# Two transformer layers on one core: weights in blocked layout, raw blocks read from the inputs, and part of one feed-forward step by seven products

## The chip, the cores and the metric

The kernel runs on one core of one Trainium2 chip. The metric is the device time of one execution in microseconds (us). The core has TensorE (PE, matrix products; its loads of the stationary operand are listed as PEld), VectorE (DVE), ScalarE (ACT), GpSimd (POOL, used only at the start) and SyncE (SP), which issues nearly all DMAs in program order from one queue; 16 DMA engines carry them out. PSUM has eight banks of 128 x 512 float32.

## The reference

The input x has 2048 rows of 1024 features. Two layers with the same weights are applied one after the other; each is an attention part and a feed-forward part, both with a layer norm ahead and a residual around:

```python
def _A_ref(x, wqkv, wo):                      # attention, 32 heads of 32
    qkv = (x @ wqkv).reshape(B, S, 3, H, Dh) ...
    off = jnp.arange(8) * 2                   # position s sees s, s-2, ..., s-14
    logits = einsum("bhsd,bhswd->bhsw", q, kg) * scale   # masked below 0
    o = einsum("bhsw,bhswd->bhsd", softmax(logits), vg)
    return o... @ wo

def _B_ref(x, w1, b1, w2, b2):                # feed-forward, 1024 -> 3584 -> 1024
    r = max(x @ w1 + b1, 0)
    return (r * r) @ w2 + b2

for _ in range(2):
    x = x + _A_ref(_layernorm(x), wqkv, wo)
    x = x + _B_ref(_layernorm(x), w1, b1, w2, b2)
```

All inputs are bfloat16. The products take float16 or bfloat16 operands and accumulate in float32.

## The kernel before

**Units.** The rows are split by even and odd position (so that the window of the attention is contiguous) and then into blocks of 512. A layer has four such blocks, so there are eight units, u = 0 to 7. A unit passes through these stages, each a method: SA (load four tiles of x, layer norm, transposed by DMA or, in unit 0, by PE), the projections Q, K, V, S2 (attention on DVE, ACT and a few matmuls `lg` against a constant `grp`), the output projection by wo with residual and the second layer norm, FFN1 and FFN2.

**Plain and by seven products.** A product of 512 rows is done in one of two ways. Plainly: matmuls of 512 columns, accumulated over the contraction in a PSUM bank. Or by Strassen's scheme in Winograd's form: the operands are cut in 2 x 2 blocks, and seven block products take the place of eight. Each product of FFN1, Q, K or V is then eight matmuls of 256 columns (`product`, L623, matmul at L633). They need sums and differences of activations (`rhs_combos`, tiles T and TA, made by DVE) and of weights. The products are numbered 1 to 7: numbers 1, 2 and 4 use raw weight blocks, 5, 7, 6 and 3 the four combinations s1, s3, s2, s4.

**How it is split.** Q, K and V are plain in units 0 and 1 (`SQ`, L871; the first four of K in unit 0 in halves at L858) and by seven products from unit 2 (`SQ7`). The output projection is plain in units 0, 1 and 7 (`SW`, L1053) and by seven in units 2 to 6 (`SW7`, L1124). FFN1 is plain in unit 0 (`SF1_plain`: seven blocks `dp` of four 512-column results each; L1195, relu L1203, square L1206) and by seven later (`SF1`, `ffn1_step`). FFN2 is plain in unit 0 (`SF2_plain`, L460, into all eight PSUM banks at once, each seeded with the bias by ACT at L473) and by seven later (`SF2`, L1336).

**Where the weights come from.** The plain units load them from the inputs with strided row pieces. While their weights are in SBUF, the kernel makes what the later units need and stores it to DRAM scratch: `keep_wqkv` makes the four combinations of each block on DVE (L521) from views with a stride of eight elements, copies the three raw blocks on ACT (L516, tiles `tr`), and stores all seven; `keep_w1` (L662), `keep_w2` (L433) and `keep_wo` (L1077) make combinations on DVE in tiles `tv`. The raw blocks of w1 are copied from DRAM to DRAM by 21 DMAs (`copy_w1`). `seven` then loads the scratch (`w1s`, `wqk`, `wqqv`) in tiles of four products, in the order in which they are used: one DMA of 1 MB for four products. FFN2 by seven loads combinations from `tw` and raw blocks from the input, seven pieces of 512 columns to a row. The stationary operands of Q, K and V have a stride of eight elements (plain) or two (by seven).

**FFN1 by seven, one block.** For each `dp`, `ffn1_step` uses three PSUM banks X, Y, Z. ACT copies X to Y (L571), copies X twice as `u` (in units of FOLD with the bias, L1244, two instructions each; otherwise L1240) and Z twice as `y` (L1250), takes four relus (L1277) and two squares (L1271); DVE adds u and y (L1254) and takes the maximum with zero (L1263 in units of FOLD, otherwise with the bias, L1267).

**Denominators.** In S2, `norm` sums the eight exponentials with three DVE additions (L980 to L982), or, for units in DEN, with eight matmuls by the identity in a PSUM bank; ACT takes logarithm and exponential of it.

**Order of the work.** `build` lists the operations with their data, priorities and cost estimates. `Plan.schedule` is a list scheduler: it takes, for each engine, the ready operation with the lowest priority number whose buffers are free, and the order that results is the fixed program order of each engine. ORDER holds seeds of small random shifts of the priorities; each list is one more pass. Buffers are slots of a class with a cap for each tag: 12 slots of 8 KB for a partition (`8K`; at most 8 of them weights `w`), four tiles `tv`, and so on. A DMA issue is planned at 0.08 us of SP.

Of the kernel before, what the change touches and what calls it, by code (L numbers as in the profile page):

```python
# [27 lines left out]
FOLD = (1, 2)  # L28
DEN = ()
# [20 lines left out]
NEARLY = 4  # L50
PR1 = 20.0
# [261 lines left out]
class _Kernel:  # L313
    def __init__(self, ctx, tc, x, wqkv, wo, w1, b1, w2, b2, out, n_layers=2):
# [4 lines left out]
        self.F = w1.shape[-1]  # L319
# [13 lines left out]
    def setup(self):  # L333
# [27 lines left out]
        self.wqkv_v = self.wqkv.rearrange("(kt p) n -> p kt n", p=128)  # L361
        self.wo_v = self.wo.rearrange("(p c) n -> p c n", c=self.NCH)
        self.w1_v = self.w1.rearrange("(kt p) n -> p kt n", p=128)
        self.w2_v = self.w2.rearrange("(kt p) n -> p kt n", p=128)
# [11 lines left out]
        self.wqs = {j: [tc.dram_tile([128, min(4, len(o) - i), 4, 256], F16, name=f"wq{j}{i // 4}") for i in range(0, len(o), 4)]  # L376
                    for j, o in self.orderq.items()}
        self.two = [tc.dram_tile([128, 2, 4, BLK], F16, name=f"two{i}") for i in range(2)]
        self.w1s = [tc.dram_tile([128, min(4, len(self.order1) - i), 4, 256], F16, name=f"w1s{i // 4}") for i in range(0, len(self.order1), 4)]
# [33 lines left out]
    def weights(self, ap, kt, wide=False):  # L413
        b = Buf("8K", "w", [128, 8, 512], BF)
        if wide:
            self.dma(lambda: b[:].rearrange("p (a b) n -> p a (b n)", a=4), lambda: ap, (), [(b, 0)], 1.19, name="w")
        else:
            self.dma(lambda: b[:, :kt, :], lambda: ap, (), [(b, 0)], kt * 0.145, name="w")
        return b

    def w2_block(self, k2, n2):
        h = self.KF // 2
        return self.w2_v[:, k2 * h:(k2 + 1) * h, n2 * BLK:(n2 + 1) * BLK]

    def keep_w2(self, j0, n, w):
# [3 lines left out]
        def raw(k2, n2):  # L429
            return w[:, k2, :n, n2 * BLK:(n2 + 1) * BLK]  # L430
# [9 lines left out]
    def SF2_plain(self, u):  # L440
# [7 lines left out]
        for j0 in range(0, h, 2):  # L448
            n = min(2, h - j0)
            w = Buf("8K", "w", [128, 2, 2, 2 * BLK], BF)  # L450
            for k2 in range(2):
                self.dma(lambda w=w, k2=k2, n=n: w[:, k2, :n], lambda k2=k2, j0=j0, n=n: self.w2_v[:, k2 * h + j0:k2 * h + j0 + n, :],
                         (), [(w, k2)], n * 0.285, name="w")
# [41 lines left out]
    def keep_wqkv(self, nm, ws, after=()):  # L495
# [4 lines left out]
        def one(s):  # L500
            at = {pr: i for i, (d, pr) in enumerate(self.orderq[job]) if d == (nm, s)}
# [1021 lines left out]
```

## Time and profile before

| what | value |
|---|---|
| three runs, median (lowest to highest) | 1143.3 us (1142.36 to 1145.3) |
| the profiled execution, its own time | 1144.01 us |
| its span | 1142.3 us |
| granted PE clock | 1.00 throughout |
| PE, PEld, DVE, ACT busy | 1128.2, 764.0, 1002.6, 804.6 us |
| bytes moved by DMA | 372.54 MB, 326 GB/s on the mean |
| packets | 208172, of these 68426 under 512 B and 147146 under 2 KB |

How it is read: the busy time of an engine is the sum of its instructions; matmuls overlap by their tails, so the rate of PE is taken from runs of many matmuls, not from the mean duration of one. A gap in brackets is time in which an engine did nothing, with what released it at the end. In the stretches, each line is a window of the span with the busy time and count of each engine. The queue q1 is the one that SP issues on; its share is the time that its packets took, over 16 engines and the span, and can exceed 1.0 in a window since packets overlap.

### The profile page before, as it was taken

What the parts mean: (1) busy time and instruction counts of PE and PEld (TensorE: products, weight loads), DVE (VectorE), ACT (ScalarE), POOL (GpSimd) and SP (SyncE); (2) the same over time, 40 slices, a digit from 0 to 9 for tenths busy, and PEclk for the clock granted to TensorE, in tenths of its full rate; (3) what the DMA queues carried; (4) which work ended last, traced back from release to release, by engine and by line L of the source; (5) the groups of instructions that cost most, each with busy time, mean ns of one, the idle gap of its engine ahead of it and who ended that gap; (6) DMA issues with size and microseconds to landing.
All of it is one profiled execution on the core that took longest, in us unless ns stands there. A gap on an engine that the chain in (4) does not pass through costs nothing.

```text
span 1142.3 us, 20183 instructions
## 1 busy us (share of the span) xinstructions
PE 1128.2 (99%) x7618; PEld 764.0 (67%) x7663; DVE 1002.6 (88%) x1513; ACT 804.6 (70%) x1574; POOL 1.8 (0%) x8
## 2 busy tenths in 40 slices
PE   8999999999999999999999999999999999999998
PEld 6665544568846788468874688647885578845864
DVE  7999999999997899959999699996999889996341
ACT  6965694367994689757895579946798477943861
POOL 0000000000000000000000000000000000000000
PEclk9999999999999999999999999999999999999999
DMA  9999998999999996999979998899979999688982
GB/s 347 330 311 313 328 297 274 308 358 355 392 356 375 371 372 227 338 350 349 387 275 331 409 342 299 293 339 391 360 265 311 370 369 381 242 317 275 365 296 77
DMA packets 208172, 372.54 MB, mean 326 GB/s; under 512 B 68426, under 2 KB 147146, under 8 KB 187594
## 3 DMA queue, kind: packets, MB, share of 16 engines
q1 hardware_dynamic: 207786, 370.72, 94.8%
q8 instruction: 60, 0.98, 0.3%
q10 hardware_dynamic: 288, 0.52, 0.1%
q14 instruction: 38, 0.31, 0.1%
HBM read 320.35 MB, written 41.68 MB: 317 GB/s over the span
## 4 chain that ended last, share of the span: by engine, by line
PE 68%; ACT 13%; DMA 6%; DVE 2%; issue 1%; SPq 0%; DVEq 0%; ACTq 0%
PE X L633 22%; PE Z L633 11%; PE X L1336 10%; PE Y L633 6%; PE Z L1336 5%; PE py L460 4%; PE X L1124 3%; PE py L1053 2%; PE Y L1336 2%; ACT r L1271 2%; DMA xt<-xs 2%; DMA w<-in_A_wo_dram 2%; PE Z L1124 2%; ACT rr L1277 1%; ACT r L1203 1%; ACT xn L727 1%
## 5 line engine op out<-in xcount | busy, mean ns | idle before, releaser
L633 PEld LDWEIGHTS <-w 128*128 128x128 f16 (+1 forms) x4760 | 465.7, 98 | 68.7 <-issue 0.5
L1336 PEld LDWEIGHTS <-r 128*128 128x128 f16 x1183 | 115.7, 98 | 135.7 <-issue 2.1
L1336 PE MATMUL X<-w,r 128*128 128x512 f16 (+2 forms) x784 | 177.7, 377 | 1.6 <-ACT yxa L1029 1.2
L922 DVE TENSOR_TENSOR P<-q,k 128x2048 f16<-128x2048 f16 x128 | 153.9, 1225 | 3.2 <-ACT q L848 1.6
L633 PE MATMUL X<-T,w 128*128 128x256 f16 x1176 | 147.0, 273 | 0.0
L1001 DVE TENSOR_TENSOR pr<-pb,v 128x4096 f16<-128x4096 f16 x64 | 146.3, 2295 | 0.3
L930 DVE TENSOR_TENSOR P<-P,P 128x2048 f16<-128x2048 f16 x106 | 129.5, 1222 | 0.3
L1008 DVE TENSOR_TENSOR pr<-pr 128x2048 f16<-128x2048 f16 (+1 forms) x128 | 119.0, 953 | 0.0
L1271 ACT ACTIVATE r<-rr 128x1024 f16<-128x1024 f16 x98 | 112.5, 1165 | 0.1
L633 PE MATMUL X<-TA,w 128*128 128x256 f16 x864 | 108.2, 273 | 0.2 <-ACT u L589 0.2
L571 ACT COPY Y<-X 128x512 f32<-128x512 f32 x109 | 67.5, 619 | 34.0 <-PE X L633 29.8
L871 PE MATMUL pq<-xnA,w 128*128 128x512 f16 x352 | 78.4, 379 | 0.0
L871 PEld LDWEIGHTS <-w 128*128 128x128 bf16 x352 | 50.3, 144 | 25.1
L1250 ACT CAST y<-Z 128x512 f16<-128x512 f32 x98 | 61.8, 648 | 3.7 <-PE Z L633 3.4
L1254 DVE TENSOR_TENSOR rr<-u,y 128x512 f16<-128x512 f16 x98 | 40.7, 422 | 22.0 <-ACT y L1250 11.1
L593 ACT CAST yq<-Z 128x512 f16<-128x512 f32 x72 | 41.8, 588 | 21.6 <-PE Z L633 18.8
L589 ACT CAST u<-X 128x512 f16<-128x512 f32 x72 | 42.0, 587 | 19.2 <-PE X L633 17.3
L1277 ACT ACTIVATE rr<-X,b1T 128x256 f16<-128x256 f32 x98 | 51.5, 583 | 0.5 <-PE X L633 0.3
L1277 ACT ACTIVATE rr<-Y,b1T 128x256 f16<-128x256 f32 x98 | 49.2, 539 | 3.5 <-PE Y L633 3.3
L633 PE MATMUL Z<-xnB,w 128*128 128x256 f16 x392 | 50.8, 273 | 0.0
L460 PE MATMUL py<-w,r 128*128 128x512 bf16 x219 | 48.9, 379 | 1.3 <-ACT py L473 0.9
L633 PE MATMUL Z<-T,w 128*128 128x256 f16 x392 | 50.1, 273 | 0.0
(153 smaller groups left out, 1727.1 us busy)
## 6 DMA issues: line engine op xcount, KB each, us to landing
w<-w1s SPq DMA_DIRECT2D x84, 1024.0 KB, 10.2
w<-tw SPq DMA_DIRECT2D x56, 896.0 KB, 6.4
w<-wqqv SPq DMA_DIRECT2D x42, 1024.0 KB, 10.4
w<-in_B_w_dram SPq DMA_DIRECT2D x42, 896.0 KB, 6.7
w<-wqk SPq DMA_DIRECT2D x18, 1024.0 KB, 9.2
w<-in_B_w_dram SPq DMA_DIRECT2D x28, 512.0 KB, 7.3
w<-in_A_wqkv_dram SPq DMA_DIRECT2D x12, 1024.0 KB, 11.2
w<-in_A_wo_dram SPq DMA_DIRECT2D x11, 1024.0 KB, 8.4
```

The source lines that it names most:

```text
L460: nc.tensor.matmul(bank[:], r2[:, k2 * h + j0 + j, tl * 128:(tl + 1) * 128], w[:, k2, j, n2 * BLK:(n2 + 1) * BLK], start=False, stop=(j0 + ...
L571: self.p.add("ACT", act(512), lambda: self.nc.scalar.copy(Y[:], X[:]), [(X, 0)], [(Y, 0)], UP, name="u")
L633: nc.tensor.matmul(bank[:, a, :], lw[:, k, left(a)], rhs(k), start=(start and k == 0 and a == 0), stop=(k == 3), skip_group_check=True)
L871: nc.tensor.matmul(pq[:], wv[:, kd % 4, c0:D:8], xnT[:, :, kd, :], start=(kd == 0), stop=(kd == KD - 1))
L922: nc.vector.tensor_tensor(cur[:], q[:, c, None, hb * HB:(hb + 1) * HB].to_broadcast([128, W, HB]), _win_ap(k[:, c, :], HALO + hb * HB, HB) ...
L930: nc.vector.tensor_tensor(other[:], other[:], cur[:], ALU.add)
L1001: p.add("DVE", dve(4096), lambda pr=pr, ch=ch: nc.vector.tensor_tensor(pr[:], pb[:].unsqueeze(1).to_broadcast([128, 2, W, HB]), _win_ap2(v ...
L1008: nc.vector.tensor_tensor(dst, pr[:, :, 0:n, :], pr[:, :, n:2 * n, :], ALU.add)
L1250: p.add("ACT", act(512), lambda: nc.scalar.copy(y[:], bank[:]), [(bank, 0)], [(y, 0)], 1.5, name="y")
L1271: p.add("ACT", 0.955, lambda: nc.scalar.activation(out=r2[:, f:f + 2, :].rearrange("p a t -> p (a t)"), in_=r[:].rearrange("p a m t -> p ( ...
L1277: p.add("ACT", 0.36, lambda a=a: nc.scalar.activation(out=r[:, a, 0, :], in_=bank[:, a, :], func=ACTF.Relu, bias=self.b1T[:, f + a:f + a + ...
L1336: nc.tensor.matmul(banks[q][:, lo:hi], left(jj, q), w[:, j, lo:hi], start=(start and jj == 0), stop=(jj == h - 1), skip_group_check=True)
```

## The change

- **Layout of the weights.** The host permutes wqkv, wo, w1 and w2 before the launch (`_lay`; it moves elements and computes nothing), so that every block that the kernel loads lies in long runs: 8 KB to a partition for half of Q, K or V, 4 KB for half a block of w1, 7 KB for half a block of w2, 4 KB or 8 KB for wo. In SBUF the operands of Q, K and V are then packed: the strides of eight and two are gone, from the matmuls' stationary operands and from the combinations in `keep_wqkv`.
- **Raw blocks.** The ACT copies at L516, their stores, and `copy_w1` are removed. The scratch holds combinations only. `seven` loads each raw block of a tile with its own DMA of 256 KB from the input (2 KB to a partition) and the combinations of the tile with one more; a product waits for its own piece, not for the whole tile.
- **FFN1 of unit 0.** Blocks 0 to 3 remain plain (PLAIN1 = 4); blocks 4 to 6 are done by seven products, with T from `rhs_combos`, the combinations taken from the tiles `tv` while they are also stored, and the raw blocks from the loaded tile.
- **Constants.** FOLD gets unit 0 (it has an `ffn1_step` now). DEN is (0,): the denominators of unit 0 are summed by PE.
- **ORDER** has new seeds, three lists in place of four. A branch in `build` for other settings of QU and K7 changes nothing with the settings here.

```diff
-FOLD = (1, 2)
-DEN = ()
+FOLD = (0, 1, 2)
+DEN = (0,)
+PLAIN1 = 4
+RAW = {1: (0, 0), 2: (0, 1), 4: (1, 1)}
 ORDER = [
...
@@ keep_wqkv
-                return ws[k][:].rearrange("p (a b) (n c) -> p a (b n) c", a=4, c=8)[:, :, :, 4 * m + 2 * s:4 * m + 2 * s + 2]
-            for pr, m, k in ((1, 0, 0), (2, 0, 1), (4, 1, 1)):
-                t = Buf("2K", "tr", [128, 4, 256], BF)
-                p.add("ACT", 1.06, lambda t=t, m=m, k=k: nc.scalar.copy(v4(t), raw(m, k)), [(ws[k], 0)], [(t, 0)], 30.0, after, name="trc")
-                store(pr, t, BF)
+                return ws[k][:, 2 * m + s]
...
@@ seven
-        for j, (d, pr) in enumerate(order):
-            if j % 4 == 0:
...
-                self.dma(lambda w=w, n=n: w[:, 0:n], lambda j=j: store[j // 4][:], [(k, i) for i in range(n)], [(w, 0)], n * 0.256,
-                         after=[spare] if sp else (), name="w")
+        for d, pr in order:
+            t, i, nr = at[d, pr]
+            if t not in ws:
+                w = ws[t] = Buf("8K", "w", [128, 4, 4, 256], F16)
+                mine = [(j, e) for e, (s, j, _) in at.items() if s == t]
+                for j, (e, q) in mine:
+                    if q in RAW:
+                        self.dma(lambda w=w, j=j: w[:, j].rearrange("p k n -> p (k n)"), lambda e=e, q=q: raw(e, *RAW[q]), (), [(w, j)], 0.256,
+                                 name="w", cast=BF)
+                cs = [j for j, (e, q) in mine if q not in RAW]
+                if cs:
+                    self.dma(lambda w=w, a=nr, b=nr + len(cs): w[:, a:b], lambda t=t: store[t][:], [(key + (t,), j) for j in cs],
+                             [(w, j) for j in cs], len(cs) * 0.256, name="w")
...
@@ qkv_step
-            bank, fm = self.product(pr, w, wi, rhs, X, Y, Z, lambda a: slice(a, 256, 2))
-            self.state[u]["gate" + nm] = p.add("PE", 8 * MMH, fm, rc + [(w, 0)], [(bank, 0)], self.nxt(), name="fq")
+            bank, fm = self.product(pr, w, wi, rhs, X, Y, Z)
+            self.state[u]["gate" + nm] = p.add("PE", 8 * MMH, fm, rc + [(w, wi)], [(bank, 0)], self.nxt(), name="fq")
...
-    def copy_w1(self, after):
...
@@ SF1_plain
-        for dp in range(self.NDP):
-            w = Buf("8K", "w", [128, 2, 8, 256], BF)
-            for m in range(2):
-                self.dma(lambda w=w, m=m: w[:, m], lambda m=m, dp=dp: self.w1_v[:, :, m * (F // 2) + dp * 256:m * (F // 2) + (dp + 1) * 256],
-                         (), [(w, m)], 0.66, name="w")
+        def load(dp):
+            w = Buf("8K", "w", [128, 2, 8, 256], BF)
+            for m in range(2):
+                self.dma(lambda m=m: w[:, m].rearrange("p k n -> p (k n)"), lambda m=m: self.w1[dp * 128:(dp + 1) * 128, m * 2048:(m + 1) * 2048],
+                         (), [(w, m)], 0.53, name="w")
+            return w
+        for dp in range(PLAIN1):
+            w = load(dp)
...
+        rhs = self.rhs_blocks(xnT, self.rhs_combos(xnT, -60.0, "8K", "T"))
+        self.ffs, steps = st["phs"], {}
+        for i, (dp, pr) in enumerate(self.interleave(range(PLAIN1, self.NDP))):
+            if dp not in steps:
+                w = load(dp)
+                steps[dp] = w, self.keep_w1(dp, w), self.ffn1_step(r2, dp, u in FOLD)
+            w, s, step = steps[dp]
+            if pr in s:
+                step(pr, s[pr], None, *rhs[pr])
+            else:
+                m, k = RAW[pr]
+                step(pr, w, (m, k), *rhs[pr])
+            if i % 7 == 6:
+                yield
...
+def _lay(name, a):
+    if name == "A_wqkv":
+        a = a.reshape(2, 4, 128, 3, 128, 4, 2).transpose(3, 0, 2, 5, 1, 6, 4).reshape(768, 4096)
+    elif name == "A_wo":
+        a = a.reshape(128, 8, 2, 512).transpose(2, 0, 1, 3).reshape(256, 4096)
+    elif name == "B_w1":
+        a = a.reshape(8, 128, 2, 7, 256).transpose(3, 1, 2, 0, 4).reshape(896, 4096)
+    elif name == "B_w2":
+        a = a.reshape(2, 14, 128, 2, 512).transpose(0, 3, 2, 1, 4).reshape(512, 7168)
+    return a
```

More of the change, by code (lines that the diff above doesn't have):

```diff
@@ L411, in par_tile, with wqkv_block, wqkv_raw, w1_raw @@
         return par_ap[cls, a0:a0 + 128, :]
[L413 to L419, printed above, removed]
-    def w2_block(self, k2, n2):
-        h = self.KF // 2
-        return self.w2_v[:, k2 * h:(k2 + 1) * h, n2 * BLK:(n2 + 1) * BLK]
+    def wqkv_block(self, nm, kh):
+        i = 2 * "qkv".index(nm) + kh
+        return self.wqkv[i * 128:(i + 1) * 128]
+    def wqkv_raw(self, d, m, k):
+        nm, s = d
+        return self.wqkv_block(nm, k)[:, (2 * m + s) * 1024:(2 * m + s + 1) * 1024]
+    def w1_raw(self, dp, m, k):
+        return self.w1[dp * 128:(dp + 1) * 128, m * 2048 + k * 1024:m * 2048 + (k + 1) * 1024]
+    def w2_block(self, k2, n2):
+        i = 2 * k2 + n2
+        return self.w2[i * 128:(i + 1) * 128]
+    def cells(self, order):
+        at = {}
+        for j in range(0, len(order), 4):
+            part = order[j:j + 4]
+            raw = [d for d in part if d[1] in RAW]
+            for i, d in enumerate(raw + [d for d in part if d[1] not in RAW]):
+                at[d] = j // 4, i, len(raw)
+        return at
+    def scratch(self, tc, order, name):
+        n = [0] * (-(-len(order) // 4))
+        for (d, pr), (t, i, r) in self.cells(order).items():
+            n[t] += pr not in RAW
+        return [tc.dram_tile([128, max(c, 1), 4, 256], F16, name=f"{name}{t}") for t, c in enumerate(n)]
     def keep_w2(self, j0, n, w):
```

133 lines of the change are left out of this document (66 added, 67 removed), and 16 rows, old and new, of the table ORDER.

## The prediction

> **What bounds the kernel now.** I read the page first: busy shares, DMA queue line, costliest groups.
>
> ```profile
> span 1142.3 us, 20183 instructions
> PE 1128.2 (99%) x7618; PEld 764.0 (67%) x7663; DVE 1002.6 (88%) x1513; ACT 804.6 (70%) x1574; POOL 1.8 (0%) x8
> ...
> q1 hardware_dynamic: 207786, 370.72, 94.8%
> ```
>
> TensorE (PE) is busy nearly throughout, and its busy time is real work: counting matmuls in the code gives 2764 of 512 columns at 0.2157 us (rate of the long runs: 49 in 10.74 us less the tail) and 4760 of 256 columns at 0.1092 us (16 in 1.75 us), 596 + 520 us, plus 6 us of start-up matmuls and 4 us of transposes, 1126 us. So time can only come from fewer columns or from PE's gaps, 14.1 us in all. Of those, 1.1 lie ahead of the first matmul and 3.8 behind the last (last adds and stores); the 45 matmul records that are missing (7663 loads, 7618 matmuls) leave about 0.05 us each, 2.4. Some 6.8 us are true gaps. Next, PE in order of time, where the bracket is the gap and its releaser (start, length in us):
>
> ```profile
> 16.13 0.18 PE L1430 MATMUL pk<-ident,b1r 28*128 28x28 f16 x1 [0.43 <-DMA b1r<-in_B_b_dram]
> 60.95 1.02 PE L937 MATMUL lg<-P,grp 128*128 128x512 f16 x4 [0.41 <-DVE P L930]
> 93.73 3.61 PE L1053 MATMUL py<-w,o 128*128 128x512 bf16 x16 [0.69 <-ACT py L473]
> 169.15 1.89 PE L1195 MATMUL ph<-xnB,w 128*128 128x512 f16 x8 [0.33 <-ACT r L1203]
> 172.53 1.89 PE L460 MATMUL py<-w,r 128*128 128x512 bf16 x8 [0.63 <-ACT py L473]
> 174.73 45.29 PE L460 MATMUL py<-w,r 128*128 128x512 bf16 x204 [0.31 <-ACT py L473]
> 232.89 1.02 PE L1053 MATMUL py<-w,o 128*128 128x512 bf16 x4 [0.67 <-DMA w<-in_A_wo_dram]
> 615.08 1.24 PE L1336 MATMUL X<-w,r 128*128 128x512 f16 x5 [0.85 <-ACT yxa L1029]
> 885.58 2.75 PE L1336 MATMUL X<-w,r 128*128 128x512 f16 x12 [0.34 <-ACT yxa L1029]
> ```
>
> The reader sees that nearly every gap of size lies before 235 us, where unit 0 and unit 1 are done plainly and the weights' copies are made. What fills the other engines there is seen in the stretches (length, then busy PE, PEld, DVE, ACT, POOL, clock, DMA share, GB/s):
>
> ```profile
> 20.00:113.00 93.00, 91.80 (x440) 57.24 (x441) 90.92 (x101) 68.40 (x122) 0.00 (x0) 1.00 1.06 324
> 113.00:170.00 57.00, 56.47 (x288) 28.21 (x287) 55.98 (x72) 45.73 (x91) 0.00 (x0) 1.00 1.00 312
> 170.00:222.00 52.00, 50.72 (x236) 23.46 (x240) 50.74 (x59) 19.68 (x38) 0.00 (x0) 1.00 0.87 291
> ```
>
> DVE is full from 20 to 222 us, and the DMA engines up to 170; ACT is nearly full while FFN1 of unit 0 runs and nearly idle behind it. Around 93 us the order of instructions shows the cause of one gap, and the chain of waits shows DMA landings ahead of the later ones:
>
> ```profile
> 90.04 2.19 ACT L516 COPY tr<-w 128x1024 bf16<-128x1024 bf16 x2
> ...
> 93.09 0.59 ACT L473 CAST py<-xt 128x512 f32<-128x512 bf16 x1
> ```
> ```profile
> 224.40 8.45 DMA w<-in_A_wo_dram
> ...
> 599.63 7.48 DMA xt<-xs
> ...
> 875.17 6.31 DMA xt<-xs
> ```
>
> **The change, part by part.**
>
> *FFN1 of unit 0, blocks 4 to 6 by seven products.* Removed: 3 x 32 = 96 matmuls of 512 columns, 96 x 0.2157 = 20.7 us. Added: 3 x 7 x 8 = 168 of 256 columns, 168 x 0.1092 = 18.3. PE -2.4.
> ACT per block: seed 0.62, two copies y 1.30, four biased copies u 2.24 (4 x 0.56), four relus 2.24, two squares 2.33, together 8.7, against four times 0.68 + 0.63 = 5.3 plainly; three blocks +10.4 us. DVE: eight T 8 x 0.42 = 3.4, and per block two adds and two maxima 1.4, +7.7 in all. FOLD for unit 0 only puts the bias on ACT, counted here. All of it runs in the stretch where ACT has 57.0 - 45.7 = 11.3 us free and DVE 1.0; what covers it is below.
>
> *Denominators of unit 0 on PE.* 16 matmuls of 256 columns, +1.7 us; DVE loses three adds twice, 2 x (1.22 + 0.69 + 0.43) = -4.7. PE sum of both: -0.6.
>
> *Raw blocks from the inputs.* 18 ACT copies of 1.17 us go (-21 us, all between 12 and 103 us), with their 18 stores; so do the 21 DRAM-to-DRAM copies of w1. ACT: -21 + 10.4 = -10 over the kernel. On SP (the queue that issues) 39 issues go, and each tile of four products is now loaded in pieces: 49 x 3/7 = 21 raw loads for each of seven units, 18 for each of six, 255 more; net +216 at 0.32 to 0.40 us, 69 to 86 us of SP. Ahead of them SP mostly waits for buffers (135.6 us for PE X alone in its list of waits), so I price this at 0; bounds: 0, since the prefetch runs ahead, and for the loss the rival below.
>
> *Block layout.* The trace's packet records give medians of 27 ns for 512 bytes, 46 for 1024, 84 for 2048, 159 for 4096, 272 for 7168, 309 for 8192. Per load: w2 block 896 x 46 -> 128 x 272, half a w1 block 1024 x 27 -> 128 x 159, wqkv 512 x 84 -> 128 x 309, and so on; with the removed copies this takes 60 us off the 16 engines (17 from w2, 6 from w1, 3 from wqkv, 4 from wo, 18 + 12 from the copies), and the pieces put 14 to 20 back (2048 bytes at 84 ns against 77 for a quarter of 8192). Net -40 of 1083 us. The strided operands go too: 24 DVE combinations of wqkv from 1.11 to 0.69 us (the row of the same shape on packed w1), -10.1; the loads of strided weights into PE from 144 to 98 ns, priced at 0, since beneath a 512-column matmul of 216 ns they hide, and even the 256-column ones ran 24 in 2.84 us, 0.11 each. DVE over the kernel: +7.7 - 4.7 - 10.1 = -7.1.
>
> *The order of all instructions* is planned anew, so small gaps appear and vanish; its price is bounded by the gaps themselves: -6.8 if all go, and some +7 if as many again are made.
>
> *Which gaps go.* 16.13, b1r lands behind wqkv loads of 512 packets each: -0.4. 60.95, the last tree add behind a DVE that has lost eight combinations x 0.42 = 3.4: -0.4. 93.73, the seed stood behind two removed copies: -0.7. 169 to 175, 1.27 us: earlier relief on ACT and DVE lets FFN1 start earlier, its own ACT work grows by 10.4; between -1.3 and +10.4. I take -0.6, nearer the gain: ACT has 11 us free inside the stretch and 52 - 20 = 32 behind it, and four layer norms of unit 2 (4.7 us each, beginning at 130 us) can move there. 232.89, wo landed 8.45 us after issue amid stores and small packets: -0.7. 615 and 885, each behind an activation load xt of 6 to 7 us: -0.6, half. Sum of gaps -3.4.
>
> **Sum.** The profiled execution took 1144.0 us (span 1142.3 and 1.7 around it). 1144.0 - 0.6 - 3.4 = 1140.0. The median of the three runs, 1143.3, stands 0.7 below that execution, so 1139.3.
>
> **Rivals.**
> *B, the gaps move.* The plan was already short of nothing but these gaps, and behind 240 us the change alters only loads. Then PE's 0.6 is all: 1142.7. For it: the late units' ACT and DVE load is unchanged. Against: four of the gaps name a thing that is removed or shrinks.
> *C, slower: ACT at the end of unit 0's FFN1.* FFN2 of unit 0 takes all eight PSUM banks, each seeded by ACT, so what ACT is late with at about 170 us stands in front of PE. ACT's extra 10.4 us fill the 11.3 us free, and the last blocks' combinations (four buffers tv, each also held until its store has landed, 4.7 us) may come late as well. If half to all of the 10.4 is uncovered, 7.8, and the other front gaps go (-2.2): 1143.3 - 0.6 - 2.2 + 7.8 = 1148.3. It is slower beyond doubt from 6.2 us uncovered. Against: the unit's start moves ahead and V's projection of unit 1, 64 matmuls or 13.8 us with little ACT work, can fill.
> *D, the small loads arrive late.* In the seven-product stages the DMA share is already 1.0, and four products take PE 3.5 us. A tile's 1 MB takes 128 x 309 / 16 = 2.5 us of the engines, in pieces 2.6; SP's issues grow from one to 2.6, about 1 us per tile. If the prefetch collapsed, the added 14 to 20 us of engine time would be the price, less nothing: 1157 to 1163, say 1158. Against it speak these rows (count, KB each, us from issue to landing): a quarter-size load of the same tensor lands no earlier, so landing is queueing ahead of need, and the total falls by 40 us.
>
> ```profile
> w<-w1s SPq DMA_DIRECT2D x84, 1024.0 KB, 10.2
> ...
> w<-w1s SPq DMA_DIRECT2D x7, 256.0 KB, 11.3
> ```
>
> The Trainium skill, page "DMA: Bandwidth & Descriptors", section "Rules for kernel authors", speaks for D: it asks for transfers of 1 MiB and over and for joining small ones. Estimated from that page's fit of 2.0 us plus bytes at 436 GB/s, a tile's pieces one after another would take 7.9 us against 4.4 whole, more than PE's 3.5, so by the rule D would decide; the rows above don't bear out that the fixed part adds up.
>
> **How the numbers follow.** A measurement of this kernel can tell about 0.3%, 3.4 us, from no change (three runs spread by 2.9). Chances: forecast 0.55 (own range 1136 to 1139.9: 1136 is 1143.3 less 0.6 and 6.8); B 0.27 (1139.9 to 1146.7); C 0.12; D 0.06. So faster 0.55, same 0.27, slower 0.18. The range reaches from 1136 to 1147, where C begins, and leaves out C's and D's greater part.
>
> **What would show it.** PE's busy time near 1127.5, and the gaps at the b1 matmul, the first lg and the first py of unit 0 and the first py of unit 1 gone. No ACT copies of w; wqkv combinations at 0.69 us. q1's share near 91% with some 15 MB less. For C: gaps of several us ahead of the first L460 matmul, released by ACT. For D: PE gaps released by DMA w in the seven-product stages. What would make me wrong above all: new gaps behind 240 us from the new order, which no row of before can show.

## The result, and the profile after

The changed kernel takes 1158.3 us (median of ten runs, 1149.67 to 1164.23) against 1144.4 us (1142.36 to 1148.06) for the kernel before on the same chip: 1.0113 times as long, with the interval 1.0088 to 1.0138. The forecast was 1139.3 us. Ratios here are of runs in the faster of two states of the chip; of the runs below only one, of e5_pool's four, was in the slower, and it is left out. The profiled execution took 1155.16 us, its span 1152.5. From its page (busy times, the queue of SP, the chain that ended last):

```profile
span 1152.5 us, 20584 instructions
PE 1130.1 (98%) x7707; PEld 756.6 (66%) x7751; DVE 993.4 (86%) x1527; ACT 797.2 (69%) x1571; POOL 1.8 (0%) x8
...
q1 hardware_dynamic: 174778, 360.51, 92.9%
...
PE 73%; DVE 12%; DMA 11%; ACT 2%; issue 2%; SPq 1%; DVEq 0%; ACTq 0%
```

PE's gaps rose from 14.1 to 22.4 us of the span, and DMA's share of the chain from 6% to 11%. The stretches of the prediction (length, then busy PE, PEld, DVE, ACT, POOL, clock, DMA share, GB/s), with the next one added:

```profile
20.00:113.00 93.00, 92.89 (x476) 45.56 (x476) 88.72 (x110) 48.03 (x95) 0.00 (x0) 1.00 0.76 248
113.00:170.00 57.00, 56.95 (x361) 34.99 (x361) 56.83 (x80) 45.30 (x82) 0.00 (x0) 1.00 0.73 254
170.00:222.00 52.00, 51.79 (x267) 26.33 (x270) 49.47 (x61) 33.04 (x66) 0.00 (x0) 1.00 1.06 305
222.00:420.00 198.00, 188.36 (x1366) 135.03 (x1370) 170.84 (x262) 137.92 (x280) 0.00 (x0) 0.98 1.02 335
```

In the kernel before, the last of them reads

```profile
222.00:420.00 198.00, 196.81 (x1478) 145.03 (x1484) 184.88 (x283) 148.71 (x300) 0.00 (x0) 1.00 1.04 370
```

So the front, where most of before's gaps lay, is now better than before: in 20 to 222 us PE (TensorE) stands still for 0.4 us, where it was 3.0. From 222 us on, with the DMA engines as full as ever, they deliver 335 GB/s in place of 370, and PE is busy for 8.4 us less by 420 us. PE in order of time (start, length, and in brackets the gap and its releaser):

```profile
228.91 1.02 PE L1069 MATMUL py<-w,o 128*128 128x512 bf16 x4 [1.63 <-DMA w<-in_A_wo_dram]
272.10 1.89 PE L657 MATMUL Z<-T,w 128*128 128x256 f16 x8 [2.11 <-DMA w<-w1s]
373.62 1.25 PE L657 MATMUL X<-TA,w 128*128 128x256 f16 x8 [2.20 <-DMA xm<-in_A_x_dram]
420.38 0.82 PE L657 MATMUL Z<-T,w 128*128 128x256 f16 x6 [2.27 <-DVE T L694]
556.67 1.03 PE L657 MATMUL Z<-T,w 128*128 128x256 f16 x8 [1.18 <-DVE T L694]
692.85 1.03 PE L657 MATMUL Z<-T,w 128*128 128x256 f16 x8 [1.22 <-DVE T L694]
```

Weights, activations and wo come late; where DVE's T is named, T itself waited for a transpose. A second profile of the changed kernel (e0_after, below) has gaps in the same places, of other lengths: 0.8 and 0.9 us at 229 and 271, 1.7, 3.1, 2.1 and 3.6 us at 373, 419, 557 and 698. What SP does ahead of the gap at 420 us shows how a transfer comes late (start, time to the end of the group's last issue, what it issues):

```profile
398.90 1.77 SPq L402 DMA_DIRECT2D w<-in_B_w_dram  x2
400.73 0.42 SPq L402 DMA_DIRECT2D w<-w1s  x1
401.25 0.38 SPq L402 DMA_DIRECT2D w<-in_B_w_dram  x1
401.67 0.43 SPq L402 DMA_DIRECT2D w<-w1s  x1
402.14 1.14 SPq L402 DMA_DIRECT2D w<-in_B_w_dram  x2
403.32 0.74 SPq L402 DMA_DIRECT2D w<-w1s  x1
404.16 3.94 SPq L767 DMA_TRANSPOSE xnB<-xn  x1
```

Eight pieces of weight tiles go out, then the transpose for which T waits; it lands 10.99 us later (chain of waits: `404.16 10.99 DMA xnB<-xn`), where the median is 7.0. Of this, 3.7 us is a wait for DVE; then the pieces issued ahead of it land first, the last at 412.7 us, and DVE stands still for it:

```profile
415.44 0.43 DVE L694 TENSOR_TENSOR T<-xnB 128x512 f16<-128x512 f16 x1 [3.84 <-DMA xnB<-xn]
```

There is also a limit on how many DMAs can be in flight. The compiled program gives SP's DMAs eight completion semaphores (counters that tell of a landing) in turn, so that SP can't issue a DMA before the one eight issues back has landed. The trace bears this out: where the landing is known, none of 730 issues of the changed kernel begins before the one eight back has landed, while the one seven back is still in flight at 326 of 731 (before: at 71 of 548). At the gap at 420 us itself this limit was not what held the transpose: the DMA eight issues back had landed at 402.9 us. SP's list of waits (what, us in total, times, longest), its dearest entries for DMA landings, first of before and then of after:

```profile
SPq L405 <- DMA w<-wqqv: 14.8, 8, 3.4
SPq L405 <- DMA w<-w1s: 13.7, 6, 3.1
SPq L405 <- DMA w<-two: 9.0, 7, 2.1
```
```profile
SPq L402 <- DMA w<-w1s: 55.3, 53, 1.8
SPq L402 <- DMA w<-in_B_w_dram: 39.6, 92, 1.7
SPq L402 <- DMA w<-wqqv: 22.8, 23, 1.5
```

Summed over all tensors, SP waited on landings for 56 us in 43 waits before and for 203 us in 283 waits after, with 633 DMAs before and 842 after; 41 of the 43 and 279 of the 283 are for the DMA eight issues back.

### The profile page after: what moved, and what is told of

Its sections match the earlier page's. It is cut to its first block, busy times and chain, and to the rows that moved or that the text cites. A ratio compares the mean times of both kernels' runs of the same rounds, so it can differ in the third digit from the quotient of the medians.

```text
span 1152.5 us, 20584 instructions
## 1 busy us (share of the span) xinstructions
PE 1130.1 (98%) x7707; PEld 756.6 (66%) x7751; DVE 993.4 (86%) x1527; ACT 797.2 (69%) x1571; POOL 1.8 (0%) x8
## 4 chain that ended last, share of the span: by engine, by line
PE 73%; DVE 12%; DMA 11%; ACT 2%; issue 2%; SPq 1%; DVEq 0%; ACTq 0%
PE X L657 20%; PE X L1373 14%; PE Z L657 10%; PE Z L1373 7%; PE pq L884 6%; PE Y L657 5%; PE Y L1373 3%; DVE P L935 3%; PE py L1069 3%; DMA xnB<-xn 3%; PE X L1140 2%; DVE P L943 2%; PE lg L950 2%; DMA w<-wqqv 1%; PE Z L1140 1%
## 5 line engine op out<-in xcount | busy, mean ns | idle before, releaser
L657 PEld LDWEIGHTS <-w 128*128 128x128 f16 (+1 forms) x4832 | 473.2, 98 | 80.1 <-issue 9.1
L657 PE MATMUL X<-T,w 128*128 128x256 f16 x1200 | 150.3, 273 | 0.0
L1021 DVE TENSOR_TENSOR pr<-pr 128x1024 f16<-128x1024 f16 (+1 forms) x128 | 117.9, 952 | 0.0
L1308 ACT ACTIVATE r<-rr 128x1024 f16<-128x1024 f16 x104 | 116.1, 1129 | 1.2 <-DVE rr L1300 0.4
L1287 ACT CAST y<-Z 128x512 f16<-128x512 f32 x104 | 64.4, 638 | 12.6 <-PE Z L657 12.4
L884 PEld LDWEIGHTS <-w 128*128 128x128 bf16 x352 | 34.4, 98 | 38.9
L657 PE MATMUL Y<-xnB,w 128*128 128x256 f16 x416 | 53.1, 273 | 0.0
L657 PE MATMUL X<-xnB,w 128*128 128x256 f16 x416 | 52.6, 273 | 0.0
```

The lines of the kernel that those rows point to most:

```text
L657: nc.tensor.matmul(bank[:, a, :], lw[:, k, a * 128:(a + 1) * 128], rhs(k), start=(start and k == 0 and a == 0), stop=(k == 3), skip_group_ ...
L884: nc.tensor.matmul(pq[:], w[kd // 4][:, c0 // 2, kd % 4, c0 % 2 * 128:c0 % 2 * 128 + 128], xnT[:, :, kd, :], start=(kd == 0), stop=(kd == ...
L1021: nc.vector.tensor_tensor(dst, pr[:, :, 0:n, :], pr[:, :, n:2 * n, :], ALU.add)
L1287: p.add("ACT", act(512), lambda: nc.scalar.copy(y[:], bank[:]), [(bank, 0)], [(y, 0)], 1.5, name="y")
L1308: p.add("ACT", 0.955, lambda: nc.scalar.activation(out=r2[:, f:f + 2, :].rearrange("p a t -> p (a t)"), in_=r[:].rearrange("p a m t -> p ( ...
```

## The experiments

Three theories to begin with. W: the number of small loads costs, through the wait for the eighth issue back. O: the new order costs. K: the smaller packets cost. Later S came up: the sizes or sources of the pieces cost. A ratio is always to the kernel before on the same chip.

**One load per tile, in the new order** (e1_one_load).

```diff
+  (kept)   21 + 18 DMAs copy the raw blocks from the inputs into the scratch tiles
-  seven:   one DMA for each raw block, one for the combinations
+  seven:   one DMA w[:, 0:n] <- store[t] for a tile
```

> The changed kernel in its own order of instructions, but the raw blocks are copied into the scratch beside the combinations (39 DRAM-to-DRAM DMAs in the front), and from then on each tile of four products is loaded by one DMA of up to 1 MB in place of two to four. Theory W (window): every DMA issue of this program waits until the issue eight before it has landed, so pieces of 256 to 768 KB let SP keep only about half as many bytes in flight, and everything that SP issues behind them (wo, x, transposes) comes late. By W the gaps of PE at 372, 419, 555, 691 and 932 us go (about 8 of the 13 us behind 220 us), SP's waits on landings fall from about 195 to under 80 us, and the time is 1143 to 1149. Theory O (order): the new order and unit 0's FFN1 by seven make the gaps; then they stay and the time is within 4 us of the changed kernel's.

Measured: 1152.95 us, ratio 1.008 (1.0062 to 1.0097), above W's range. The gaps at 272, 373, 420, 556 and 692 us are gone and SP's waits on landings fell to 99 us, as W says; but there are new gaps of 2.2 to 3.1 us at 13, 120 and 227 us, in an order that was not made for the added copies: at 120 us the load that PE waits for stood behind three of them. Half a confirmation. With whole tiles in the new order the kernel is still 15 us above the layout alone (e4_layout, next but two), so pieces aren't the only way to lose time.

**The old kernel with its tile loads cut** (e2_split).

```diff
-  seven:   dma(w[:, 0:n], store[j // 4][:])
+  seven:   one DMA for each raw block of the tile, one for its combinations, all from store[j // 4]
```

> The kernel before in its own order of instructions; only each load of a tile of four products is cut into as many DMAs as the changed kernel has for it (one for each raw block, one for the rest), all from the same scratch. By W it gets slower by 6 to 14 us (1149 to 1158), with PE gaps behind 230 us released by DMA landings; by O, and if only the packets' size matters, it stays within 3 us.

Measured: 1150.14 us, 1.0064 (1.004 to 1.0088), inside W's range, SP's waits on landings 175 us. Pieces cost 6 us with the order, layout and bytes of before.

**Smaller packets alone** (e3_2k).

```diff
-  seven:   dma(w[:, 0:n], store[j // 4][:])          # 8 KB to a partition in one packet
+  seven:   the same DMA, in four packets of 2 KB to a partition
```

> The kernel before, one DMA for each tile as it was, but the scratch is laid out so that every packet of these loads has 2 KB in place of 8 KB. If the slower packets matter (theory K, 16 engines busier by some 30 us for all 98 units of four blocks), it is slower by 5 us or more; by W and O it stays within 3 us.

Measured: 1145.33 us, 1.0016 (1.0003 to 1.0028). K falls as an explanation of 14 us, although the DMA engines did get busier: each worked for 1124 us (98.0% of a span of 1146.7) in place of 1083. More time of the DMA engines alone is thus not yet more time of the kernel.

**The layout alone** (e4_layout, and e4_again).

```diff
+  _lay: the host's permutation; all plain loads, stationary operands and combinations as in the changed kernel
   seven, copy_w1, ACT copies, ORDER, FOLD, DEN, FFN1 of unit 0: as before
```

> The kernel before in its own order of instructions, with the blocked layout of the weights alone: long packets for wqkv, w1, w2 and wo, packed operands; raw blocks are still copied by ACT and by DMA to the scratch, FFN1 of unit 0 is plain. By W and O alike the layout by itself does no harm: 1139 to 1144, with the gap at 232.9 us (wo) shorter. If the layout itself were the cause, it would be slower by 5 us or more.

> The kernel before with the blocked layout alone, once more, on the chip of this call's other kernels, as the measure for them: 1136 to 1139 us.

Measured: 1137.56 us, 0.9945 (0.993 to 0.9959); again 1137.63 us, 0.994 (0.9925 to 0.9955). It beats both kernels, and lies below the 1139 to 1144 us that W and O allowed. PE's gaps of over 0.4 us that are left behind the first matmul:

```profile
8.23 1.35 PE L790 MATMUL pt<-ident,xn 128*128 128x128 f16 x16 [1.45 <-DVE xn L772]
15.40 0.18 PE L1435 MATMUL pk<-ident,b1r 28*128 28x28 f16 x1 [0.49 <-DMA b1r<-in_B_b_dram]
```

PE is as busy as before, 1128.2 us, and its gaps fell from 14.1 to 7.9 us. Those at 93, 169 to 175, 233, 615 and 885 us, which closed, are 3.8 of these 6.2 us; about 2.4 were, by the prediction's reckoning, records that are missing before and here are not (7663 matmuls for 7663 loads), so that part of the gain has no place in the trace. SP's waits on landings are 93 us, more than before's 56, in the faster kernel.

**Raw pieces through a queue of their own** (e5_pool), beside the changed kernel again (e0_after).

```diff
-  raw pieces: self.nc.sync.dma_start(...)
+  raw pieces: self.nc.gpsimd.dma_start(...)       # 255 issues, completion semaphores of GpSimd's own
```

> The changed kernel again, on the chip of this call's other kernels, as the measure for them. All theories: 1150 to 1164 us, with the stretches without TensorE work near 229, 272, 374 and 420 us.

> The changed kernel, operation for operation and in its order; only the queue of the loads that take raw blocks from the inputs changes: GpSimd issues them, with completion semaphores of its own. Sizes, bytes and the order of the work stay. Theory W (SP waits for the landing of the eighth issue back, so that many small loads shorten the reach of the prefetch): SP has about 250 issues fewer to get through and the waits of SP on landings fall from 203 us to under 120; the gaps at 272, 374 and 420 us go or halve, 1143 to 1152 us. Theory S (the smaller sizes themselves keep the transfers from coming in time): nothing moves, 1154 to 1162. Theory O (the new order is what costs): nothing moves either.

Measured: e0_after 1159.11 us, 1.013 (1.0085 to 1.0175); e5_pool 1227.16 us, 1.0717 (1.0662 to 1.0772), far outside every theory. SP's waits on landings did fall, to 112 us, but the urgent transfers land later. The transposes' rows (count, median us to landing), first of the changed kernel, then of e5_pool, with the queue that GpSimd issues on and one of its gaps:

```profile
xnA<-xn SPq DMA_TRANSPOSE x28, 6.9
xnB<-xn SPq DMA_TRANSPOSE x28, 7.0
```
```profile
xnA<-xn SPq DMA_TRANSPOSE x28, 7.0
xnB<-xn SPq DMA_TRANSPOSE x28, 14.2
...
q0 software_dynamic: 20400, 66.86, 18.0%
...
883.79 1.44 PE L657 MATMUL Z<-T,w 128*128 128x256 f16 x6 [12.93 <-DVE T L694]
```

One reading is that the wait of eight cuts both ways: it holds issues back, and it keeps the queue short for what is urgent; with a second issuer more is in flight, and the transposes wait behind it. This is not shown: the pieces also moved to a queue of another kind (software_dynamic), and no run separates the two. W has in any case to be put more narrowly. SP's waits as such don't cost (the layout alone has more of them than before and is faster); what costs is a DMA that PE needs soon and that comes late behind others. The Trainium skill, page "DMA: Bandwidth & Descriptors", section "Rules for kernel authors", says that spreading DMAs over issuing engines brings no bandwidth, since all share the same 16 engines and interleave there; here it lost 68 us, with one of the two kinds of transposes landing after twice the time.

**Raw pieces in before's order** (e6_raw, e6_again).

```diff
   e4_layout, and in addition
-  ACT copies, their stores, copy_w1
+  seven: raw blocks one by one from the inputs, combinations from the scratch
```

> Before's order with the blocked layout (1137.6 us alone), and now the raw blocks straight from the inputs: no copies on ScalarE, no copies from memory to memory, and a tile's load in pieces (SP has 888 DMAs instead of 633). All stretches of TensorE work are as before. Theory W: the pieces cost here what they cost under the old layout (6.2 us), or a little less since 10 MB and some 20 ScalarE copies go: 1141 to 1147 us, waits of SP on landings at least 150 us. Theory O (the new order or unit 0's change costs, loads in pieces do not): 1136 to 1139 us.

> e6_raw again, on the chip of this call's other kernels: 1153 to 1160 us.

Measured: 1157.36 us, 1.0112 (1.0083 to 1.0142); again 1158.19 us, 1.012 (1.0075 to 1.0166). That is within 2 us of the changed kernel's time, without its order, its products for unit 0 and its denominators on PE. So O isn't needed for the 14 us; that another order costs nothing is not shown, for with whole tiles e1_one_load and e7_seven (below) lose time too. It is also 20 us above the layout alone, above W's range, which went by the 6 us of e2_split: something more than the number costs here.

**The changed kernel, order made anew with the wait built in** (e8_window).

```diff
   schedule:
                 if o.mb:
+                    lands.append(end + o.lat)
+                    if len(lands) >= 8:
+                        efree[e] = max(efree[e], lands[-8])
   ORDER: seeds searched for this schedule
```

> The changed kernel's operations and loads, all of them, pieces and unit 0's products too; only the order is made anew, by a list schedule that lets SP issue no DMA before the landing of the one eight issues back. That schedule's own span is 1134.9 us (the changed kernel's own schedule, which lets SP run ahead without end, had 1134.1 us and took 1152.5). Theory W: the loads that came late are asked for earlier, and the gaps at 272, 374 and 420 us go; 1138 to 1148 us. Theory S (the sizes themselves): 1152 to 1160 us whatever the order.

Measured: 1147.04 us, 1.0031 (1.0018 to 1.0045), inside W's range; the same loads, the same 842 DMAs, 12 us less than the changed kernel. The gaps at 374 and 420 us are gone, and of the one at 272 us 0.9 us is left, at 269.

```profile
span 1143.4 us, 20576 instructions
PE 1126.7 (99%) x7702; PEld 755.0 (66%) x7751; DVE 994.9 (87%) x1527; ACT 793.8 (69%) x1571; POOL 1.8 (0%) x8
```

SP's waits on landings are nearly those of the changed kernel (196 us); what differs is the order, and with it what stands behind these waits. Two things weaken the run as evidence for W: its ORDER has 1109 seeds where the changed kernel's has 92, and no order searched as long without the wait of eight was run beside it.

**Unit 0's products with one load per tile** (e7_seven).

```diff
   e4_layout, and in addition FFN1 of unit 0, FOLD and DEN as in the changed kernel
+  raw blocks copied from memory to memory in unit 0; one DMA for a tile; ORDER searched with the wait of eight
```

> The blocked layout, part of unit 0's FFN1 by seven products and its combinations on VectorE as in the changed kernel, but a tile's load stays one DMA: the raw blocks are copied from memory to memory in the unit-0 stage. Order made anew with the wait of eight built in (its span 1136.6 us). Theory W: with pieces gone the kernel is near the blocked layout alone, 1134 to 1143 us; the part for unit 0 is worth its products, about 2 us, less what its copies cost. Were unit 0's part itself what costs, over 1147 us.

Measured: 1149.19 us, 1.0026 (1.0008 to 1.0044), 12 us above the layout alone: above W's range, where a cost of unit 0's part itself was to be seen. But its gaps are

```profile
54.91 0.59 PE L1001 MATMUL lg<-P,grp 128*128 128x512 f16 x2 [2.82 <-DVE P L994]
...
121.37 1.79 PE L695 MATMUL X<-xnB,w 128*128 128x256 f16 x8 [2.46 <-DMA w<-in_B_w_dram]
277.85 1.28 PE L695 MATMUL X<-xnB,w 128*128 128x256 f16 x8 [3.77 <-DMA w<-w1s]
```

and two of the three wait for weights. The changed kernel, which has unit 0's products without the copies and another order, has nothing like the first two, and at 272 us one like the third. What these products are worth by themselves isn't told by this run: inconclusive. It does show that whole tiles and an order made with the wait of eight don't by themselves reach the layout alone.

**Number of issues alone** (e9_tiny, e10_small).

```diff
   e4_layout, and behind a tile's load, for each raw block in it:
+  e9_tiny:   dma_start(tinies[i:i + 1], b1[0:32])                  # 64 bytes
+  e10_small: dma_start(tinies[i, :, 0:256], w1[0:16, 0:256])       # 16 rows of 512 bytes
```

> The blocked layout alone, in before's order, with one 64-byte DMA from memory to memory behind a tile's load for every raw block in the tile: 255 DMAs more on SP's queue, next to no bytes; sizes, sources and number of the loads themselves stay. Theory W (what costs is the number of issues, each of which holds one of eight places until it lands): as with the raw pieces, 1150 to 1160 us, waits of SP on landings over 150 us, late transposes and wo loads. Theory S (what costs is the smaller pieces, or where they are read from): 1137 to 1140 us.

> The blocked layout alone, in before's order, with 255 further small DMAs behind the tile loads as in e9_tiny, but each of 16 rows of 512 bytes (8 KB, one row for each DMA engine; e9_tiny's 64 bytes went as 32 packets of 2 bytes, 8,160 of them, and loaded the engines by some 240 us of their 1,320). At the 27 ns that a 512-byte packet takes in the trace these are 7 us of each engine's time. Sizes and sources of the loads stay. Theory W (the number of issues, each of which holds one of eight places until it lands): 1146 to 1160 us, waits of SP on landings over 150 us. Theory S (the smaller pieces themselves or where they are read from): 1137 to 1141 us.

Measured: e9_tiny 1321.52 us, 1.1542 (1.1524 to 1.1561), outside both theories. By the trace's packet records each 64 bytes went as 16 packets of 4 bytes, with 16 more of 4 bytes that every DMA has.

```profile
DMA packets 153230, 372.59 MB, mean 282 GB/s; under 512 B 76586, under 2 KB 84906, under 8 KB 131242
```

Of these 68,426 under 512 bytes are the layout's own; 8,160 more are 255 times 32 (the expectation of e10_small takes them for 32 packets of 2 bytes). The queue's share of its span is 98.6%, some 240 us of each engine above the layout alone (98.6% of 1321.3 against 93.5% of 1136.1 us). This time doesn't stand in the added packets, whose median is 9 ns, but mostly in the 8-KB packets of the tile loads, whose mean rose from 327 to 484 ns, 216 us for each engine. Why so is open, and the run tells nothing of the number of issues alone. e10_small: 1143.42 us, 0.9994 (0.9983 to 1.0006), 5.8 us above the layout alone; SP's waits on landings are 199 us. It lies below W's range and above S's: the number alone costs, but less than the whole; wo and T are late:

```profile
767.43 1.02 PE L1134 MATMUL X<-w,o 128*128 128x512 bf16 x3 [0.91 <-DMA w<-in_A_wo_dram]
...
1058.87 1.03 PE L641 MATMUL Z<-T,w 128*128 128x256 f16 x8 [0.64 <-DVE T L688]
```

The 255 issues add SP's own issuing time (0.32 to 0.40 us each by the prediction's rows) as well as 255 places taken among the eight, and the run doesn't tell these two apart.

**Pieces, and where they are read from** (e11_split4, e11_again, e12_keep, e13_input, e14_form).

```diff
   e4_layout, and in addition
+  e11: a tile's load in the pieces of e6_raw, all from its scratch tile
+  e12: e11, but the raw pieces from the inputs (copies still made, nobody reads them)
+  e13: loads whole; FFN1's 91 tiles from 1-MB areas of the input w1
+  e14: e12, but raw pieces from scratch tensors [128, 4096] of the inputs' form, into which the copies go
```

> The blocked layout alone, in before's order, with every tile's load cut into just the pieces of e6_raw, but all of them read from the scratch tensors, whole tiles of them: raw copies, stores and all bytes stay. Against e6_raw (1157.4 us) it tells the pieces from where the raw blocks are read. Theory W (number of issues): as e6_raw, 1150 to 1160 us. If the raw blocks cost because they are read from the inputs: 1143 to 1147 us, the 6 us that pieces cost under the old layout.

> e11_split4 again, on the chip of this call's other kernels: 1143 to 1153 us. If it comes within 3 us of e6_again, the 12 us between the two were the chip's or the run's.

> e6_raw with what it had dropped put back: the raw blocks are still copied (by ScalarE and from memory to memory) and stored to scratch as in before, but nobody reads those copies; the raw blocks are loaded from the inputs. If reading the inputs is what costs the 12 us between e6_raw and e11_split4: 1153 to 1160 us. If it is that 39 transfers dropped out of SP's order (the bulk loads behind them come earlier and stand before urgent ones): 1143 to 1148 us. Theory W by itself (number of issues) has no difference between the three, about 8 us over the layout alone: 1143 to 1150 us.

> The blocked layout alone, in before's order, one DMA per tile; only the source of FFN1's 91 tile loads changes: whole 1-MB areas of the input w1, of the same shape and pitch, instead of the scratch tensors (so FFN1's weights are not the right ones; every operation and byte stays, and the scratch is still written). If the input tensors are slower to read by themselves: the engines' time for the same packets rises by 1 to 3%, and the time by 2 to 12 us, to 1140 to 1150 us. If they are not, and the 12 us between e12_keep and e11 need the small pieces as well: 1136 to 1139 us.

> e12_keep with one thing changed: the raw blocks are read from scratch tensors that have the form of the inputs (128 rows of 4,096, one tensor for each block row), into which unit 0's copies now go, instead of from the inputs. Number, sizes, order and shape of the pieces are e12_keep's, the tensor read is scratch as in e11_again. If something about small pieces of the input tensors costs the 14 us: 1143 to 1150 us. If it is the form, with a tile's raw pieces in other places of memory than its combinations: 1156 to 1164 us.

Measured: e11_split4 1145.75 us, 1.0025 (1.0007 to 1.0043), e11_again 1147.56 us, 1.0039 (1.0024 to 1.0053); e12_keep 1161.55 us, 1.0156 (1.0137 to 1.0176); e13_input 1138.6 us, 0.9948 (0.9931 to 0.9964); e14_form 1154.3 us, 1.008 (1.0051 to 1.0108). SP's queue (packets, MB, share of the 16 engines), in the order e11_again, e12_keep, e14_form, each with its span:

```profile
span 1145.8 us, 20523 instructions
...
q1 hardware_dynamic: 194442, 370.74, 95.1%
```
```profile
span 1160.4 us, 20523 instructions
...
q1 hardware_dynamic: 194442, 370.74, 96.5%
```
```profile
span 1160.1 us, 20523 instructions
...
q1 hardware_dynamic: 194442, 370.74, 96.2%
```

The packets and bytes are equal to the last one, yet each engine worked for 1090, 1120 and 1116 us (span times share). Cutting the loads costs 8 to 10 us of the end time (both e11 runs fall below W's range and near that of the rival in its expectation, that the source costs the rest). Reading the raw pieces from tensors other than the one that holds the tile's combinations costs more at the end: 14 us from the inputs (e12_keep against e11_again on the same chip; 1.6 us above the highest range of its expectation, that of the inputs), 5 to 7 us from scratch of the inputs' form (e14_form against e11_again, by ratio and by time; between the two ranges of its expectation). The intervals of e12_keep and e14_form lie apart, though e14_form's five runs spread over 1151.8 to 1161.8 us and its profile is of the slowest of them. So the form costs a part, and small pieces out of the inputs seem to cost a further part (the two ran on different chips); the inputs as such are not slow, since whole tiles from them cost 1 us (e13_input, which has the wrong weights in FFN1, with every operation and byte in place).

The 30 us of engine time are not the measure of this. By the packet records about 12 of them stand in the 2-KB packets (mean 93.2 against 95.5 ns), and 15 in the 57,372 packets of 256 bytes (29.4 against 33.6 ns), which are the transposes' (56 of 256 KB make 57,344) and read no weights; the changed kernel and e8_window, with the same loads in two orders, differ by 10 us of each engine (1071 and 1061). What makes the arrangement dearer stays open.

## Why the prediction was wrong

**The failed step** is "net +216 at 0.32 to 0.40 us, 69 to 86 us of SP. Ahead of them SP mostly waits for buffers ..., so I price this at 0", and with it rival D's dismissal: "a quarter-size load of the same tensor lands no earlier, so landing is queueing ahead of need". The pieces were priced at nothing; they cost 8 to 10 us when cut from one tensor (e11 against e4_layout) and 20 us as the change reads them (e6_raw against e4_layout, in the same order). The row was right and its reading wrong. A quarter of the size doesn't land in a quarter of the time, here either (count, KB each, median us to landing; e4_layout, then e11_split4):

```profile
w<-w1s SPq DMA_DIRECT2D x84, 1024.0 KB, 10.0
```
```profile
w<-w1s SPq DMA_DIRECT2D x175, 256.0 KB, 7.0
```

With eight DMAs in flight and no more, that is a reason why size matters: eight whole tiles are 8 MB in 10.0 us, far more than the 328 GB/s that the kernel moves on the mean, while eight quarters are 2 MB in 7.0 us, some 300 GB/s (an estimate from these two rows; a real stretch mixes sizes), less than it needs. By this estimate whole tiles let SP load ahead of need, and pieces don't. That the limit of eight makes the 8 to 10 us, and not SP's own issuing time, is argued and not shown: SP's DMA instructions, waits for data within them included, take 400 us in e4_layout and 521 us in e11_again, so both grew together. SP's free time, 135.6 us of waits for PE X, was no measure of it: those waits halved (67 us), and SP still had them.

The Trainium skill's page "DMA: Bandwidth & Descriptors", section "Rules for kernel authors", which asks for 1 MiB and over for each DMA and for joining small ones, was weighed and put aside; e4_layout and e11_split4 (whole, and cut, 8 to 10 us apart) agree with it. The prediction's estimate from that page, pieces one after another, isn't how it came about: pieces overlap, up to eight of them. (That fit is the page's for DMAs issued by GpSimd, and these are SP's; with the prediction's 2.6 issues for a tile it comes to 7.6 us, not 7.9.)

**The sum, by the runs** (medians, us):

| step | forecast | measured | from |
|---|---|---|---|
| layout alone | part of the gaps' -3.4 | -6.4 (again: -7.1) | e4_layout, e4_again against before |
| loads in pieces | 0 | +8 to +10 | e11 against e4 |
| raw pieces from tensors apart | not seen | +14 | e12_keep against e11_again |
| copies and their stores dropped | part of the gaps | -3.4 | e6_again against e12_keep |
| unit 0's products, denominators, new order | -0.6 and gaps | +1.8 | e0_after against e6_raw |

1144.4 - 6.4 + 9 + 14 - 3.4 + 1.8 = 1159.4, against 1158.3 measured. The rows lead from one run to the next, from before to the changed kernel, so that the sum comes out is no proof of them; they give the sizes in this order of steps. In another order they would differ: the new order with whole tiles (e1_one_load) is 15 us above the layout alone, not 1.8. The last row joins two things: the new order had gaps of its own in place of others.

**Point by point.** The gaps at the b1 matmul, the first lg, the first py of unit 0 and at the junction of FFN1 and FFN2 did go, as forecast, and rival C (ACT at the end of unit 0's FFN1) did not come: 113 to 222 us has 0.3 us without PE. But the layout alone closes most of these, to which the prediction gave the copies and the junction as reasons; its worth, priced only through the gaps, was put too low. The gaps at 615 and 885 us, of which half was counted, both went with the layout. In the changed kernel the wo gap did not go: it grew from 0.67 to 1.63 us. PE's work, -0.6, can't be read from the busy time of after, which holds stretches at a lower clock; at full clock (e8_window) it is 1126.7, -1.5. DVE fell by 9.2 (forecast 7.1), ACT by 7.4 (10). SP's DMAs rose by 209 (forecast 216), and the bytes on q1 fell by 10 MB (forecast 15). The engines' time was to fall by 40 us: it fell from 1083 to 1071. The layout gave 21 (e4_layout, 1062) where 30 were summed, the pieces took 27 where 14 to 20 were summed, and 30 more came with the raw pieces' places; dropping the copies (e6_raw, 1080) and the new order gave 40 and 9 back.

Rival D had the mechanism in part right, loads that come late, and its "say 1158" is the time that was measured. That number is luck: D got it by adding 14 to 20 us of engine time, and in the changed kernel the engines' time fell by 12.

"New gaps behind 240 us from the new order, which no row of before can show" was named as what could make the forecast wrong: the place was right, and the order as such is not needed for it, since before's order loses as much (e6_raw). A schedule that knew the wait of eight, from a longer search, took 12 us off the changed kernel without changing a load.

## What to carry to other kernels

Count the DMAs in flight before cutting a load: with a fixed number of completion semaphores, what is in flight is at most that number times the size, and a landing time that doesn't shrink with size is a warning, not a comfort. What a smaller load delays is often not itself but the urgent transfer queued behind it, so look at the landing of transposes and of first tiles; a second issuing engine made that worse here, not better. A schedule made for one pattern of loads has to be made anew with the issue limit in it when the pattern changes, and changes of layout and of loading are best measured one by one: here one alone was worth 0.55% and the other cost 1.7% (e6_raw over e4_layout).

## What was not expected of the hardware

Two of the gaps, of 2.1 and 2.2 us, came with a lowered granted clock: 0.50 for 3.4 us from 271.9 and from 374.3 us (columns as in the stretches above):

```profile
260.00:280.00 20.00, 17.84 (x149) 14.90 (x147) 16.24 (x28) 11.31 (x22) 0.00 (x0) 0.91 1.03 289
360.00:380.00 20.00, 17.58 (x127) 12.81 (x127) 7.53 (x16) 10.29 (x19) 0.00 (x0) 0.91 0.96 354
375.00:376.00 1.00, 0.78 (x3) 0.36 (x3) 0.45 (x2) 0.49 (x1) 0.00 (x0) 0.50 0.96 387
```

A mean of 0.91 over 20 us is worth up to 1.8 us of PE's work beside the gap itself. The gap of 2.27 us at 420 us was followed by no such stretch, so the length of the gap alone doesn't decide it. The same 194,442 packets took each engine 1090 or 1120 us, and half of the difference stands in transposes that were not changed. With 255 DMAs of 64 bytes among them, the 8-KB packets took half as long again on the mean (e9_tiny). And the times spread differently: the changed kernel's ten runs over 14.6 us, those of before over 5.7, those of the layout alone over 1.4 and 2.0 (four runs each); but e11_again, with late loads, has five runs within 1.4 us.
